# Sparse attention and gated feed-forward: one piece per pair for values and next scores, with the scores in the gate's and value's banks

## The chip, the cores and the metric

The kernel runs on one core of one Trainium2 chip, in one launch. The metric is the device time of that launch in microseconds (us). TensorE does the matrix products (PE in the profile; PEld is its loading of weights), VectorE (DVE), ScalarE (ACT) and GpSimd (POOL) work element by element, and SyncE (SP) starts DMA transfers. Matmuls write to PSUM, which has eight banks of 512 fp32 columns; the other operands are in SBUF.

## The reference

Eight batches of eight heads attend over 576 positions. Four heads see the last 32 positions ("local"), four see every 32nd ("strided"). The result feeds a gated layer without a routing step.

```python
rel = pos[:, None] - pos[None, :]
mask_local = (rel >= 0) & (rel < 32)
mask_strided = (rel >= 0) & (pos[None, :] % 32 == pos[:, None] % 32)
scores = np.where(masks, q @ k.T / sqrt(64), -1e9)          # per head
attn = softmax(scores)
x = (attn @ v), heads side by side: [4608 tokens, 512]
out = (sigmoid(x @ w_gate) * (x @ w_val)) @ w_out           # 512 -> 1536 -> 512
```

All data is fp32.

## The kernel before

**Feed-forward.** The 4608 tokens are nine blocks of 512. Block `k` below 8 holds the first 512 tokens of batch `k`; block 8 holds the 64 that are left over of each batch. The hidden size 1536 is twelve chunks `f` of 128. Each chunk takes three *rounds* on TensorE: gate (`g`), value (`v`) and outputs (`o`). Every operand is split into a high and a low part (`xh`/`xl`, `wh`/`wl`, `hh`/`hl`), and three products stand for one; so a gate or value round is 4 x 3 = 12 matmuls of 128x128 by 512 columns, and an output round is 4 token groups `i` x 3 = 12 matmuls too. Gate and value have one PSUM bank each, `g` and `v`, and no second one. The four output accumulators fill two pairs of banks, `o0` (`i` = 0, 1) and `o1` (`i` = 2, 3), over all twelve chunks. The last pair of banks, `a`, is for attention.

Behind a gate round ScalarE takes tanh and exp of `g` (tiles `t`, `e`), behind a value round VectorE multiplies the sigmoid together with `v` (`e`, line 410, the only reader of the bank `v`; then `t`, line 411), ScalarE rounds the result to `hh` and VectorE takes the rest, `hl`. Line 386 clears the sign bit of `t`. The output round of a chunk stands one chunk later: gate 5, value 5, outputs 4, gate 6 and so on. When the twelfth chunk of a block is summed, ScalarE copies accumulators 0 and 2 and VectorE 1 and 3 into the buffers `ost` and `l0` (one each), and SP stores them (lines 432 to 443).

**Attention.** A *pair* is two heads of one batch, four pairs (steps 0 to 3) a batch; steps 0 and 2 are local, 1 and 3 strided. A pair's functions have letters: `Q` and `V` load, `Z` takes room, `S` computes the scores (lines 208 to 214; 40 or 24 small matmuls), `F` adds the mask and takes off the maximum, `E` exp, `N` the sum and the scaling, `B` transposes in eight pieces of 32 rows on VectorE, `X` is the product with the values (line 289), `H`, `L` and `R` split the result into `xh` and `xl` of that batch's block and keep the 64 left-over tokens.

**Order.** The first two batches' attention, block 0 and the preparation of the weights follow a table written by hand. From block 1 on, `block` sets TensorE's order: while block `k` is in its feed-forward (`k` = 1 to 6), the four pairs of batch `k + 1` are worked on in eight *pieces* between rounds. Behind gate 0, 3, 6 and 9 stand a pair's scores, behind value 2, 5, 8 and 11 its values. Both use the banks `a`. TensorE keeps the order in which the code is written; for the other engines a scheduler chooses the order when the program is built, and each then works its queue off in that order.

Of the kernel before, what the change touches and what calls it, by code (L numbers as in the profile page):

```python
# [9 lines left out]
F32 = mybir.dt.float32  # L10
F32R = mybir.dt.float32r
# [3 lines left out]
ALU = mybir.AluOpType  # L15
# [28 lines left out]
NF = DF // P  # L44
BANK = 512
BY_PE = 2
AT = (0, 7)
LATE = NF - 1

BANKS = {  # L50
# [33 lines left out]
def attention_then_glu(ctx, tc, qk_l, qk_s, v_l, v_s, w_all, consts, out):  # L84
# [21 lines left out]
    def x_tiles(b):  # L106
        xs[b] = [(odd if b % 2 else work).tile([P, NC, TB], F32R, tag=t, name=f"{t}{b}") for t in ("xh", "xl")]
# [56 lines left out]
    def pair(b, step, space):  # L164
# [30 lines left out]

        todo = {}

        def score(sc):
            qk = tiles["qk"]

            m = LB if local else QB
            for n in range(ns * (P // m)):
                s, g = divmod(n, P // m)
                q = n % (NBL if local else NG)
                for j in range(2):
                    d = slice(j * D, (j + 1) * D)
                    q0, k0 = (q * LB, S + q * LB) if local else (q * GS, SK + q * GS)
                    nc.tensor.matmul(  # L208
                        sc[g * m : (g + 1) * m, j * BANK + s * kk : j * BANK + (s + 1) * kk],
                        qk[d, q0 : q0 + m],  # L210
                        qk[d, k0 : k0 + kk],
                        start=True,
                        stop=True,
                    )
            todo["soft"] = sc.rearrange("p (j n) -> p j n", j=2)[:, :, : ns * kk]

        def soft():
            sc = todo["soft"]
            prob, row, by_row = rows()
            if local:  # L220
                to = tiles["sb"][:, : 2 * ns * kk].rearrange("p (j n) -> p j n", j=2)
                nc.vector.tensor_tensor(to, sc, mask_l.broadcast_to([P, 2, ns * kk]), op=ALU.add)
            else:
                for j in range(2):
                    to, sv = prob[:, j * ns : (j + 1) * ns], sc[:, j].rearrange("p (t k) -> p t k", k=kk)
                    nc.vector.tensor_tensor(to, sv, mask_s.broadcast_to([P, ns, kk]), op=ALU.add)
            nc.vector.tensor_reduce(row, prob, axis=AX.X, op=ALU.max)
            nc.vector.tensor_tensor(prob, prob, by_row, op=ALU.subtract)  # L228

# [106 lines left out]
    def bank(tag, name):  # L336
        return ps.tile([P, 2 * BANK], F32, tag=tag, name=name)

    def attention(b):

        x_tiles(b)
        left_over(b)
        for step in range(4):
            do = pair(b, step, work)
            do["Q"](), do["V"](), do["Z"]()
            do["S"](bank("a", f"s{b}_{step}"))
            do["F"](), do["E"](), do["N"](), do["B"]()
            yield
            do["X"](bank("a", f"x{b}_{step}"))
            do["H"](), do["L"](), do["R"]()  # L350
            yield

    def split_rest():
# [34 lines left out]
    def glu_val(k, f, v=None):  # L388
        if v is None:
            v = ps.tile([P, BANK], F32, tag="v", name=f"v{k}_{f}")  # L390
            products(v, k, f, 1)
        if k == 0:
            e, t = hs[k, f], work.tile([P, TB], F32, tag="t", name=f"t{k}_{f}")
        else:
            t, e = hs[k, f]
        hh = work.tile([P, TB], F32R, tag="hh", name=f"hh{k}_{f}", bufs=2)
        hl = work.tile([P, TB], F32R, tag="hl", name=f"hl{k}_{f}", bufs=2)
        hs[k, f] = (hh, hl)
        half = 1.0 if k == 0 else 0.5
# [10 lines left out]
        nc.vector.scalar_tensor_tensor(e, e, 1.0, v, op0=ALU.min, op1=ALU.mult)  # L410
# [5 lines left out]
    def glu_out(k, f):  # L416
        hh, hl = hs.pop((k, f))
        if f == 0:
            two = [bank(f"o{n}", f"o{k}_{n}") for n in range(NTT // 2)]
            acc[k] = [two[i // 2][:, i % 2 * BANK : (i % 2 + 1) * BANK] for i in range(NTT)]  # L420
        for i in range(NTT):
            for n, (h, w) in enumerate(((hh, wh[f][2]), (hh, wl[f][2]), (hl, wh[f][2]))):
                nc.tensor.matmul(  # L423
                    acc[k][i],
                    h[:, i * P : (i + 1) * P],
                    w,
                    start=f == 0 and n == 0,
                    stop=f == NF - 1 and n == 2,
                )
        if f < NF - 1:  # L430
            return
        for i, o in enumerate(acc.pop(k)):
            ob = (work if i % 2 else odd).tile([P, DM], F32, tag="l0" if i % 2 else "ost", name=f"ob{k}_{i}")
            if i % 2:
                nc.vector.tensor_copy(ob, o)  # L435
            else:
                nc.scalar.copy(ob, o)
            if k < B:
                nc.sync.dma_start(out[k * S + i * P : k * S + (i + 1) * P, :], ob)
            else:  # L440
                for n in range(P // REST):
                    at = (i * P // REST + n) * S + TB
                    nc.sync.dma_start(out[at : at + REST, :], ob[n * REST : (n + 1) * REST, :])

    def block(k, f, pend, last):
        for slot in range(3):
            if slot == 0:
                glu_gate(k, f)
            elif slot == 1:
                glu_val(k, f)  # L450
            elif last:
                glu_out(*last)
            if (3 * f + slot) % 9 in AT:
                next(pend, None)

    for f in range(LATE):
        weight_tiles(f)
# [55 lines left out]

    with tc.manual_schedule(engines={mybir.EngineType.PE}):
        last = (0, NF - 1)
        for k in range(1, NB):
            pend = attention(k + 1) if k + 1 < B else iter(())
# [5 lines left out]
            for _ in pend:  # L523
                pass
        glu_out(*last)


def _layouts(q, k, v, w_gate, w_val, w_out):
# [80 lines left out]
```

## Time and profile before

| | |
|---|---|
| median of 3 runs | 1005.47 us (1004.60 to 1009.63) |
| the profiled execution | 1005.63 us, of it 1003.8 us span |
| TensorE busy | 975.5 us (97%) |
| VectorE busy | 589.0 us (59%) |
| ScalarE busy | 319.8 us (32%) |
| TensorE in the chain that ended last | 91% of the span |
| mean granted TensorE clock | 0.996 |
| one outputs matmul of 512 columns, mean | 394 ns, started every 227 ns |
| large matmuls in one round | 12, 2.72 us |

A matmul's row is longer than the distance to the next matmul's start, since they overlap; the chain of waits counts a round from the end of the round before to its own last matmul's end. "MATMUL ... x72" for values counts each fp32 matmul as two. The profile's DVE rows of one softmax are spread by source line: 222 or 226 mask (local, strided), 227 maximum, 228 subtraction, 236 sum, 237 and 238 reciprocal, 239 scaling, 261 transposes.

### The profile page before, as it was taken

To read this page: it belongs to the slowest core of one execution; us is meant where nothing else is said; L and a number is where in the kernel's file an instruction comes from. 1 tells how busy PE (TensorE), PEld (TensorE's weight loads), DVE (VectorE), ACT (ScalarE), POOL (GpSimd) and SP (SyncE) were. 2 spreads that over 40 slices of the span, in tenths; PEclk is the share of its full clock that TensorE was granted. 3 is DMA by queue.
4 is the path that set the end of the run, shared out by engine and by line. 5 is a ranking of instruction groups with operands and counts; after the bars stand their busy time and mean duration, and the time that the engine had idled before them with its cause. 6 is when DMAs were issued, how large, how long until landed. Compare 5 with 4: busy or idle time off the path is not lost.

```text
span 1003.8 us, 18124 instructions
## 1 busy us (share of the span) xinstructions
PE 975.5 (97%) x7840; PEld 794.7 (79%) x7840; DVE 589.0 (59%) x1042; ACT 319.8 (32%) x635; POOL 5.3 (1%) x20
## 2 busy tenths in 40 slices
PE   4999999999999999999999999999999999999996
PEld 3787878888888888888888888888888888888885
DVE  5888876666666566656665666666665633333222
ACT  3887853222322222222222232223222322222221
POOL 0000000000000000000000000000000000000000
PEclk9999999999999999999999999999999999999999
DMA  6666632111211121101210121112110010000001
GB/s 235 231 184 208 216 109 74 35 51 41 94 41 52 41 73 62 51 21 48 84 46 31 41 94 41 52 41 83 52 52 17 1 43 1 0 7 36 1 1 42
DMA packets 19871, 66.02 MB, mean 66 GB/s; under 512 B 2256, under 2 KB 2384, under 8 KB 19792
## 3 DMA queue, kind: packets, MB, share of 16 engines
q1 hardware_dynamic: 18352, 59.28, 18.3%
q10 hardware_dynamic: 1440, 5.59, 1.7%
q8 instruction: 61, 1.00, 0.4%
q14 instruction: 18, 0.15, 0.0%
HBM read 55.42 MB, written 9.44 MB: 65 GB/s over the span
## 4 chain that ended last, share of the span: by engine, by line
PE 91%; DMA 3%; DVE 3%; ACT 2%; issue 0%; SPq 0%; ACTq 0%; DVEq 0%
PE v L369 29%; PE o L423 28%; PE g L369 27%; PE x L289 3%; PE s L208 3%; DMA raw<-in_w_all 1%; DMA qk<-in_qk_l 1%; DMA qk<-in_qk_s 1%; ACT high L139 1%; PE gv L369 0%; DVE high L149 0%; ACT low L143 0%; DVE mx L236 0%; DVE w L162 0%; ACT pt L269 0%
## 5 line engine op out<-in xcount | busy, mean ns | idle before, releaser
L423 PE MATMUL o<-w,hh 128*128 128x512 f32 x864 | 270.2, 394 | 0.0
L369 PE MATMUL v<-xh,w 128*128 128x512 f32 x784 | 262.8, 395 | 0.0
L369 PE MATMUL g<-xh,w 128*128 128x512 f32 x784 | 258.4, 390 | 0.0
L423 PEld LDWEIGHTS o<-w,hh 128*128 128x128 f32 x864 | 159.6, 188 | 35.2 <-DVE ob L435 2.1
L369 PEld LDWEIGHTS v<-xh,w 128*128 128x128 f32 x784 | 148.1, 189 | 32.9
L369 PEld LDWEIGHTS g<-xh,w 128*128 128x128 f32 x784 | 147.2, 188 | 30.9
L386 DVE TENSOR_SCALAR t<-t 128x512 int32<-128x512 int32 x96 | 41.0, 427 | 219.7 <-ACT t L383 218.9
L423 PE MATMUL o<-w,hl 128*128 128x512 f32 x432 | 168.4, 390 | 0.0
L369 PE MATMUL v<-xl,w 128*128 128x512 f32 x392 | 153.8, 392 | 0.0
L369 PE MATMUL g<-xl,w 128*128 128x512 f32 x392 | 152.7, 390 | 0.3 <-DVE xl L324 0.3
L402 ACT ACTIVATE hh<-t 128x512 fp32r<-128x512 f32 x108 | 68.3, 633 | 258.1 <-DVE t L411 256.3
L383 ACT ACTIVATE t<-g 128x512 f32<-128x512 f32 x96 | 57.4, 598 | 265.2 <-PE g L369 265.2
L410 DVE SCALAR_TENSOR_TENSOR e<-e,v 128x512 f32<-128x512 f32 x96 | 65.8, 686 | 91.2 <-PE v L369 91.2
L261 DVE STREAM_TRANSPOSE pt<-sb 32x320 f32<-32x320 f32 (+1 forms) x192 | 103.0, 536 | 3.1
L405 DVE SCALAR_TENSOR_TENSOR hl<-t,hh 128x512 fp32r<-128x512 f32 x108 | 74.6, 691 | 48.5 <-ACT hh L402 48.5
L423 PEld LDWEIGHTS o<-w,hl 128*128 128x128 f32 x432 | 81.1, 188 | 17.6 <-DVE hl L405 0.4
L369 PEld LDWEIGHTS g<-xl,w 128*128 128x128 f32 x392 | 73.6, 188 | 15.8 <-DVE xl L324 0.8
L369 PEld LDWEIGHTS v<-xl,w 128*128 128x128 f32 x392 | 74.0, 189 | 14.3
L411 DVE SCALAR_TENSOR_TENSOR t<-t,e 128x512 f32<-128x512 f32 x96 | 66.5, 692 | 3.3
L384 ACT ACTIVATE e<-g 128x512 f32<-128x512 f32 x96 | 57.0, 594 | 0.0
L232 ACT ACTIVATE sb<-sb 128x640 f32<-128x640 f32 (+1 forms) x32 | 23.8, 744 | 69.5 <-DVE sb L228 69.5
L289 PEld LDWEIGHTS x<-pt,vv 64*64 64x64 f32 (+1 forms) x1856 | 34.8, 140 | 13.7 <-issue 9.7
(60 smaller groups left out, 655.2 us busy)
## 6 DMA issues: line engine op xcount, KB each, us to landing
raw<-in_w_all SPq DMA_DIRECT2D x36, 512.0 KB, 4.2
qk<-in_qk_s SPq DMA_DIRECT2D x14, 599.0 KB, 4.2
vv<-in_v_l SPq DMA_DIRECT2D x13, 640.0 KB, 4.0
qk<-in_qk_l SPq DMA_DIRECT2D x14, 592.0 KB, 3.8
out<-ob SPq DMA_DIRECT2D x32, 256.0 KB, 2.0
vv<-in_v_s SPq DMA_DIRECT2D x13, 384.0 KB, 3.2
vv<-in_v_l ACTq DMA_DIRECT2D x3, 640.0 KB, 5.8
qk<-in_qk_s ACTq DMA_DIRECT2D x2, 599.0 KB, 4.2
```

Of the source, the lines that this page charges most:

```text
L208: nc.tensor.matmul(sc[g * m : (g + 1) * m, j * BANK + s * kk : j * BANK + (s + 1) * kk], qk[d, q0 : q0 + m], qk[d, k0 : k0 + kk], start=Tr ...
L261: nc.vector.transpose(dst[to : to + LB, :, col : col + LB], src[rows : rows + LB, :, h * LB : (h + 1) * LB])
L289: nc.tensor.matmul(xp[j * D : (j + 1) * D, r * BANK + (u * per + g) * m : r * BANK + (u * per + g + 1) * m], v[rows, (u * per + g) * P + j ...
L369: nc.tensor.matmul(o, w, x, start=first and n == 0, stop=last and n == len(todo) - 1)
L383: nc.scalar.activation(t, g, AF.Tanh, scale=0.5)
L384: nc.scalar.activation(e, g, AF.Exp)
L386: nc.vector.tensor_scalar(ti, ti, 0x7FFFFFFF, None, op0=ALU.bitwise_and)
L402: nc.scalar.activation(hh, t, AF.Copy, scale=half)
L405: nc.vector.scalar_tensor_tensor(hl, t, half, hh.bitcast(F32), op0=ALU.mult, op1=ALU.subtract)
L410: nc.vector.scalar_tensor_tensor(e, e, 1.0, v, op0=ALU.min, op1=ALU.mult)
L411: nc.vector.scalar_tensor_tensor(t, t, 1.0, e, op0=ALU.add, op1=ALU.mult)
L423: nc.tensor.matmul(acc[k][i], h[:, i * P : (i + 1) * P], w, start=f == 0 and n == 0, stop=f == NF - 1 and n == 2,)
```

## The change

1. `attention` is now one generator over all 24 pairs. A piece holds a pair's values and then the next pair's scores. It stands in blocks 1 to 6 at chunks 2, 5, 8 and 11, behind the output round of the chunk before, and that chunk's own output round follows at once. The first scores stand alone, the last values too.
2. All scores but the first go to two single banks with the tags `g` and `v`, one head each, so the banks `a` are for values alone. The local mask is added in two instructions, one for each bank. `V` is loaded behind the mask and the next pair's `Q` behind the transposes.
3. So the output round of chunk 3 (6, 9) is no longer ahead of piece and gate: behind a piece come outputs 2, gate 3, value 3, gate 4, value 4, outputs 3. `hh` and `hl` have three buffers instead of two.
4. In block 8 the output rounds of chunks 10 and 11 are done together, accumulator by accumulator, behind outputs 9; each accumulator is copied and stored when it is done, from four different buffers, and the last one in two halves by ScalarE and VectorE.

```diff
-            todo["soft"] = sc.rearrange("p (j n) -> p j n", j=2)[:, :, : ns * kk]
+            todo["soft"] = [x.rearrange("p (j n) -> p j n", n=BANK)[:, :, : ns * kk] for x in sc]
...
+    def attention():
+        todo = [(b, step) for b in range(BY_PE, B) for step in range(4)]
+        ahead, now = pair(*todo[0], work), None
+        ahead["Q"]()
+        for n, (b, step) in enumerate(todo + [(B, 0)]):
+            if now:
+                of, p = todo[n - 1]
...
+                now["X"](bank("a", f"x{of}_{p}"))
+                now["H"](), now["L"](), now["R"]()
+            if b < B:
+                now = ahead
+                now["Z"]()
+                if n == 0:
+                    now["S"](bank("a", f"s{b}_{step}"))
+                else:
+                    now["S"](*(ps.tile([P, BANK], F32, tag=t, name=f"s{b}_{step}_{t}") for t in "gv"))
+                now["F"](), now["V"](), now["E"](), now["N"](), now["B"]()
+                if n + 1 < len(todo):
+                    ahead = pair(*todo[n + 1], work)
+                    ahead["Q"]()
+            yield
...
-        hh = work.tile([P, TB], F32R, tag="hh", name=f"hh{k}_{f}", bufs=2)
-        hl = work.tile([P, TB], F32R, tag="hl", name=f"hl{k}_{f}", bufs=2)
+        hh = work.tile([P, TB], F32R, tag="hh", name=f"hh{k}_{f}", bufs=3)
+        hl = work.tile([P, TB], F32R, tag="hl", name=f"hl{k}_{f}", bufs=3)
...
+    def give_out(k, i, cut=slice(0, DM), by=None):
+        tag = ("ost", "l0", "t", "e")[i if k == B else i % 2]
...
+    def glu_out(k, *fs):
...
         for i in range(NTT):
+            for f in fs:
+                out_products(k, f, i)
+            if k == B and fs[-1] == NF - 1 and i < NTT - 1:
+                give_out(k, i)
...
+        if k == B:
+            give_out(k, NTT - 1, slice(0, DM // 2), nc.scalar.copy)
+            give_out(k, NTT - 1, slice(DM // 2, DM), nc.vector.tensor_copy)
+        else:
+            for i in range(NTT):
+                give_out(k, i)
...
         last = (0, NF - 1)
+        pend = attention()
         for k in range(1, NB):
...
             for f in range(NF):
-                block(k, f, pend, last)
-                last = (k, f)
...
+                glu_gate(k, f)
+                glu_val(k, f)
+                if last and (k, f) != (B, NF - 2):
+                    glu_out(*last)
+                    last = None
+                if (k, f) == (1, 0):
+                    next(pend)
+                if k + 1 < B and f % 3 == 2:
+                    next(pend)
+                    glu_out(k, f)
+                else:
+                    last = last or (k, f)
+        glu_out(B, NF - 2, NF - 1)
```

**VectorE around a strided pair's softmax in block 3** (pair 1 of batch 4: tiles `sb4_1`, `mx4_1`, `pt4_1`; `e3_3`, `t3_3`, `hl3_3` belong to chunk 3 of block 3). Before:

```order
L226 TENSOR_TENSOR sb4_1_4016<-s4_1_4019,cst_61 128x6x54
L227 TENSOR_REDUCE mx4_1_4017<-sb4_1_4016 128x12 [waits DVE_49]
L228 TENSOR_TENSOR sb4_1_4016<-sb4_1_4016,mx4_1_4017 128x12x54 [waits DVE_49]
L410 SCALAR_TENSOR_TENSOR e3_3_4007<-e3_3_4007,v3_3_4062 128x512 [waits PE_49,Activation_49]
L411 SCALAR_TENSOR_TENSOR t3_3_4008<-t3_3_4008,e3_3_4007 128x512 [waits DVE_49]
L236 TENSOR_REDUCE mx4_1_4017<-sb4_1_4016 128x12 [waits Activation_49]
L405 SCALAR_TENSOR_TENSOR hl3_3_4076<-t3_3_4008,hh3_3_4075 128x512 [waits Activation_49]
```

And now, at the same pair:

```order
L326 TENSOR_TENSOR xl4_3967<-x4_0_3968,xh4_3966 128x512 [waits Activation_49]
L228 TENSOR_TENSOR sb4_1_4008<-s4_1_g_4011,cst_61 128x6x54 [waits PE_49]
L228 TENSOR_TENSOR sb4_1_4008<-s4_1_v_4012,cst_61 128x6x54 [waits PE_49]
L229 TENSOR_REDUCE mx4_1_4009<-sb4_1_4008 128x12 [waits DVE_49]
L230 TENSOR_TENSOR sb4_1_4008<-sb4_1_4008,mx4_1_4009 128x12x54 [waits DVE_49]
L238 TENSOR_REDUCE mx4_1_4009<-sb4_1_4008 128x12 [waits Activation_49]
L239 TENSOR_SCALAR mx4_1_4009<-mx4_1_4009 128x12 [waits DVE_49]
L240 RECIPROCAL mx4_1_4009<-mx4_1_4009 128x12 [waits DVE_49]
L241 TENSOR_TENSOR sb4_1_4008<-sb4_1_4008,mx4_1_4009 128x12x54 [waits DVE_49]
L263 STREAM_TRANSPOSE pt4_1_4048<-sb4_1_4008 32x12x32 [waits DVE_49]
L263 STREAM_TRANSPOSE pt4_1_4048<-sb4_1_4008 32x12x32 [waits Pool_49]
L263 STREAM_TRANSPOSE pt4_1_4048<-sb4_1_4008 32x12x32 x6
```

The next two rows now are chunk 3's sign bit and the multiply that reads its value bank, which stood in the middle of the softmax before:

```order
L400 TENSOR_SCALAR t3_3_4085<-t3_3_4085 128x512 [waits Activation_49]
L424 SCALAR_TENSOR_TENSOR e3_3_4084<-e3_3_4084,v3_3_4089 128x512 [waits PE_49,Activation_49]
L425 SCALAR_TENSOR_TENSOR t3_3_4085<-t3_3_4085,e3_3_4084 128x512 [waits DVE_49]
L419 SCALAR_TENSOR_TENSOR hl3_3_4103<-t3_3_4085,hh3_3_4102 128x512 [waits Activation_49]
L400 TENSOR_SCALAR t3_4_4122<-t3_4_4122 128x512 [waits Activation_49]
```

All 23 merged pieces have this order; at the first chunk of a block two output copies of the block before stand in it as well, one ahead of the sum and one ahead of the transposes.

**TensorE at the end** (`o8_0` is the pair of banks of accumulators 0 and 1, `o8_1` that of 2 and 3). Before, the last round:

```order
L423 MATMUL o8_0_8358<-w11_2_1766,hh8_11_8844 128x512 [waits Activation_49]
L423 MATMUL o8_0_8358<-w11_2_1766,hh8_11_8844 128x512
L423 MATMUL o8_0_8358<-w11_2_1766,hl8_11_8845 128x512 [waits DVE_49]
L423 MATMUL o8_0_8358<-w11_2_1766,hh8_11_8844 128x512 x2
L423 MATMUL o8_0_8358<-w11_2_1766,hl8_11_8845 128x512
L423 MATMUL o8_1_8359<-w11_2_1766,hh8_11_8844 128x512 x2
```

Now, from accumulator 0's last three matmuls to the first of accumulator 2:

```order
L433 MATMUL o8_0_8392<-w11_2_1766,hh8_11_8866 128x512 [waits Activation_49]
L433 MATMUL o8_0_8392<-w11_2_1766,hh8_11_8866 128x512
L433 MATMUL o8_0_8392<-w11_2_1766,hl8_11_8867 128x512 [waits DVE_49]
L433 MATMUL o8_0_8392<-w10_2_94,hh8_10_8829 128x512 [waits Activation_49]
L433 MATMUL o8_0_8392<-w10_2_94,hh8_10_8829 128x512
L433 MATMUL o8_0_8392<-w10_2_94,hl8_10_8830 128x512
L433 MATMUL o8_0_8392<-w11_2_1766,hh8_11_8866 128x512 x2
L433 MATMUL o8_0_8392<-w11_2_1766,hl8_11_8867 128x512
L433 MATMUL o8_1_8393<-w10_2_94,hh8_10_8829 128x512 x2
```

The fourth row is accumulator 1's first matmul: it has a wait for ScalarE, although its operand was already used for accumulator 0. Accumulator 3's first matmul has the same.

More of the change, by code (lines that the diff above doesn't have):

```diff
@@ L46 @@
 BY_PE = 2
-AT = (0, 7)
 LATE = NF - 1
@@ L196, in pair, with score @@
         todo = {}
-        def score(sc):
+        def score(*sc):
             qk = tiles["qk"]
@@ L208, in score @@
                     nc.tensor.matmul(
-                        sc[g * m : (g + 1) * m, j * BANK + s * kk : j * BANK + (s + 1) * kk],
+                        sc[j % len(sc)][g * m : (g + 1) * m, j // len(sc) * BANK + s * kk : j // len(sc) * BANK + (s + 1) * kk],
                         qk[d, q0 : q0 + m],
@@ L337, in bank @@
         return ps.tile([P, 2 * BANK], F32, tag=tag, name=name)
[L339 to L350, printed above, removed]
+    def attention():
[5 more added lines that the diff above has]
+                of, p = todo[n - 1]
+                if p == 0:
+                    x_tiles(of)
+                    left_over(of)
+                now["X"](bank("a", f"x{of}_{p}"))
[11 more added lines that the diff above has]
+                    ahead["Q"]()
             yield
@@ L414, in attention_then_glu, with out_products @@
     acc = {}
-    def glu_out(k, f):
-        hh, hl = hs.pop((k, f))
-        if f == 0:
+    def out_products(k, f, i):
+        hh, hl = hs[k, f]
+        for n, (h, w) in enumerate(((hh, wh[f][2]), (hh, wl[f][2]), (hl, wh[f][2]))):
+            nc.tensor.matmul(
+                acc[k][i],
+                h[:, i * P : (i + 1) * P],
+                w,
+                start=f == 0 and n == 0,
+                stop=f == NF - 1 and n == 2,
+            )
+    def give_out(k, i, cut=slice(0, DM), by=None):
+        tag = ("ost", "l0", "t", "e")[i if k == B else i % 2]
+        if (k, i) not in given:
+            given[k, i] = (odd if tag == "ost" else work).tile([P, DM], F32, tag=tag, name=f"ob{k}_{i}")
+        ob, o = given[k, i], acc[k][i]
+        if by is None:
+            by = (nc.scalar.copy, nc.vector.tensor_copy)[i % 2]
+        by(ob[:, cut], o[:, cut])
+        if k < B:
+            nc.sync.dma_start(out[k * S + i * P : k * S + (i + 1) * P, cut], ob[:, cut])
+        else:
+            for n in range(P // REST):
+                at = (i * P // REST + n) * S + TB
+                nc.sync.dma_start(out[at : at + REST, cut], ob[n * REST : (n + 1) * REST, cut])
+    given = {}
+    def glu_out(k, *fs):
+        if fs[0] == 0:
             two = [bank(f"o{n}", f"o{k}_{n}") for n in range(NTT // 2)]
@@ L421, in glu_out @@
         for i in range(NTT):
[L422 to L430, printed above, removed]
-            return
[L432 to L454, printed above, removed]
+            for f in fs:
+                out_products(k, f, i)
+            if k == B and fs[-1] == NF - 1 and i < NTT - 1:
+                give_out(k, i)
+        if fs[-1] < NF - 1:
+            return
+        if k == B:
[4 more added lines that the diff above has]
+                give_out(k, i)
     for f in range(LATE):
@@ L520, in attention_then_glu @@
             for f in range(NF):
-                block(k, f, pend, last)
-                last = (k, f)
-            for _ in pend:
-                pass
-        glu_out(*last)
+                glu_gate(k, f)
[8 more added lines that the diff above has]
+                    glu_out(k, f)
+                else:
+                    last = last or (k, f)
+        glu_out(B, NF - 2, NF - 1)
 def _layouts(q, k, v, w_gate, w_val, w_out):
```

9 lines of the change are left out of this document (5 added, 4 removed).

## The prediction

> **What bounds the kernel now.** I read the page first, then the chain of waits, then the timelines of the engines around one pair, and last the end.
>
> ```profile
> span 1003.8 us, 18124 instructions
> PE 975.5 (97%) x7840; PEld 794.7 (79%) x7840; DVE 589.0 (59%) x1042; ACT 319.8 (32%) x635; POOL 5.3 (1%) x20
> PE 91%; DMA 3%; DVE 3%; ACT 2%; issue 0%; SPq 0%; ACTq 0%; DVEq 0%
> 315.08:422.97 107.89, 107.89 (x921) 87.77 (x921) 67.60 (x121) 27.94 (x59) 0.68 (x2) 1.00 0.16 53
> ```
>
> TensorE is the bound: 91% of the chain, and in the stretch of one whole token block (the last row) it is busy for all 107.89 us at full clock. That leaves two things to gain: what TensorE loses between kinds of matmuls, and the end. It also means that every wait put on TensorE is paid in full. The chain, around both kinds of pair (start, us, what):
>
> ```profile
> 226.45 1.28 PE x L289 x72
> 227.73 2.95 PE o L423 x12
> 230.68 2.72 PE g L369 x12
> 233.40 0.85 PE s L208 x48
> 234.25 2.94 PE v L369 x12
> ...
> 253.51 0.84 PE x L289 x44
> 254.35 2.94 PE o L423 x12
> ...
> 260.01 0.97 PE s L208 x64
> 260.98 2.99 PE v L369 x12
> ```
>
> A round of twelve large matmuls takes 2.72; the round behind a piece of small ones takes 2.94 to 2.99. So each piece has a toll of 0.22 to 0.27, 0.24 on average.
>
> **The saving.** Before, 48 pieces stand between rounds. Now there are 25: the first scores, 23 merged pieces, the last values. 23 tolls fall away: 23 x 0.24 = 5.5 us at most. Whether the change from values to scores inside a piece has a toll of its own no row shows (between 0 and 0.24). It turns out not to matter, because of what comes next.
>
> **The new wait.** The scores now sit in the banks of gate and value. Behind a merged piece TensorE runs: outputs, gate, value, gate, value, with no outputs between the two value rounds. The second value round writes the bank that the first filled, so it has to wait until VectorE has multiplied the first one out (`e`, line 410). On VectorE the order puts that multiply behind the entire softmax of the new pair: split, two mask additions, maximum, subtraction, sum, scaling and eight transposes. Before, the multiply of the first value round stood in the middle of the softmax. I time this queue from VectorE's and ScalarE's own rows before (start, us, ...):
>
> ```profile
> 228.54 0.57 ACT L320 CAST xh<-x 128x512 fp32r<-128x512 f32 x1
> 229.27 0.68 DVE L324 TENSOR_TENSOR xl<-x,xh 128x512 fp32r<-128x512 f32 x1
> 233.50 0.60 ACT L383 ACTIVATE t<-g 128x512 f32<-128x512 f32 x1 [3.29 <-PE g L369]
> 234.47 0.89 DVE L226 TENSOR_TENSOR sb<-s,cst 128x324 f32<-128x324 f32 x2
> 237.12 0.75 ACT L232 ACTIVATE sb<-sb 128x648 f32<-128x648 f32 x1 [2.54 <-DVE sb L228]
> 238.64 0.82 DVE L236 TENSOR_REDUCE mx<-sb 128x12 f32<-128x648 f32 x1
> 240.03 0.17 DVE L237 TENSOR_SCALAR mx<-mx 128x12 f32<-128x12 f32 x1
> 241.36 4.65 DVE L261 STREAM_TRANSPOSE pt<-sb 32x384 f32<-32x384 f32 x8
> 246.38 0.68 DVE L410 SCALAR_TENSOR_TENSOR e<-e,v 128x512 f32<-128x512 f32 x1
> ...
> 214.27 4.12 DVE L261 STREAM_TRANSPOSE pt<-sb 32x320 f32<-32x320 f32 x8
> 218.77 0.68 DVE L410 SCALAR_TENSOR_TENSOR e<-e,v 128x512 f32<-128x512 f32 x1
> ...
> 255.61 0.70 ACT L320 CAST xh<-x 128x288 fp32r<-128x288 f32 x3
> 256.34 0.82 DVE L324 TENSOR_TENSOR xl<-x,xh 128x288 fp32r<-128x288 f32 x3
> ```
>
> Pair of strided scores behind local values (12 merged pieces), in us from the start of the piece:
> - Values end at 1.28. ScalarE follows a TensorE end by 0.10 (gate ends 230.68 + 2.72 = 233.40, tanh starts 233.50), so its cast starts at 1.38, VectorE's split 0.73 later (228.54 to 229.27) at 2.11, and the mask additions a step of 0.61 to 0.68 later at 2.75. The scores have ended by then (1.28 + 0.85).
> - Mask additions to exponential: 234.47 to 237.12, 2.65. Exponential and step: 0.78. Sum and step: 0.86. Scaling: 240.03 to 241.36, 1.33. Transposes, sign bit and all, up to the multiply: 241.36 to 246.38, 5.02. The multiply: 0.69. Together 11.33: the value bank is free at 14.08.
> - TensorE comes there at 1.28 + 0.85 + 2.95 + 3 x 2.72 = 13.24.
>
> How fast TensorE goes on is seen where one round already waits for VectorE, at an output copy:
>
> ```profile
> 164.19 2.96 PE o L423 x12
> 164.72 0.69 DVE L435 COPY ob<-o 128x512 f32<-128x512 f32 x1
> ```
>
> The copy ends at 165.41 and the round at 167.15; the six matmuls that waited take 6 x 0.227 = 1.36, so in the chain's count they begin at 165.79, 0.38 after the copy. The second value round thus begins at 14.08 + 0.38 = 14.46 instead of 13.24: **1.2 us lost, 12 times, 14.6 us.**
>
> Local scores behind strided values (11 pieces): values end at 0.84, cast at 0.94, split at 1.67, mask additions at 2.48; the transposes are 0.52 shorter (214.27 to 218.77 is 4.50), so 10.8 up to the end of the multiply, 13.28, and TensorE begins at 13.66. It comes there at 0.84 + 0.97 + 2.97 + 8.16 = 12.94: **0.7 us, 11 times, 7.9 us.** A toll inside the piece would make TensorE come later and wait less; the sum stays.
>
> Five of these 11 stand at a block's end, with two output copies on VectorE ahead of the multiply. The first (0.69) fits into the wait for the exponential. The second stands ahead of the transposes and waits for the first one's store:
>
> ```profile
> 157.43 0.59 ACT L437 COPY ob<-o 128x512 f32<-128x512 f32 x1 [0.90 <-PE o L423]
> 160.23 0.59 ACT L437 COPY ob<-o 128x512 f32<-128x512 f32 x1 [1.69 <-DMA out<-ob]
> ```
>
> A buffer is back 2.2 us after its copy ended (158.02 to 160.23). VectorE's first copy ends near 5.8, the store is done at 8.0, and the scaling ends at 8.1: so only the copy itself, 0.65 us, **5 times, 3.3 us.**
>
> Nothing is late twice: behind the delayed value round come outputs and gate, 5.4 us, before the next value round asks for its bank, and VectorE's queue has only that round's own multiplies left by then. The rest I cost at nothing: the three-deep `hh` and `hl` let one round stay open and fit. Values' and scores' loads leave when their buffers come free, a pair (27 us) ahead of need, against 4 us to landing (row below); ScalarE, 32% busy, hides its part. The first scores move behind the outputs but stay in their own bank. SP takes the same loads, now within 1 us of each other.
>
> ```profile
> vv<-in_v_l SPq DMA_DIRECT2D x13, 640.0 KB, 4.0
> ```
>
> **The end.** Before:
>
> ```profile
> 993.71 0.40 PE L423 MATMUL o<-w,hl 128*128 128x512 f32 x1
> 994.15 0.59 ACT L437 COPY ob<-o 128x512 f32<-128x512 f32 x1 [2.01 <-PE o L423]
> 995.09 0.39 PE L423 MATMUL o<-w,hl 128*128 128x512 f32 x1
> 997.82 0.59 ACT L437 COPY ob<-o 128x512 f32<-128x512 f32 x1 [3.08 <-DMA out<-ob]
> 999.20 0.69 DVE L435 COPY ob<-o 128x512 f32<-128x512 f32 x1 [3.74 <-DMA out<-ob]
> L443 SPq DMA_DIRECT2D out<-ob x8: 466/562/595, 994.8 to 1000.4; - x8
> ```
>
> The third and fourth copies wait 3.08 and 3.74 us for a buffer; four buffers end that. But the first copy began at 994.15, when the second accumulator's last matmul had ended (993.71 + 0.40): waits go by the pair of banks. Now that copy stands between the two accumulators' matmuls, and in the order TensorE's next matmul waits for ScalarE. Each such stop costs (0.39 - 0.23) + 0.04 + 0.59 + 0.19 for going on = 0.98 us, and there are two. The last matmul then ends 1.9 later, at 997.4; the halves are copied one after the other (the same pair of banks) by 998.2, and four stores of 0.56 each leave from 997.8, the last at 999.5, against 1000.4 before: **0.9 us gained.** [...]
>
> **Sum.** 14.6 + 7.9 + 3.3 - 5.5 - 0.9 = +19.4 us. The profiled execution took 1005.63 (span 1003.8), the median of three 1005.47; so 1025, and I take 1024 since VectorE's steps without a wait between them overlap by up to 0.08. Half a per cent, 5 us, is about what a measurement of this kernel can tell from no change.
>
> **Rivals.**
> - *The softmax stays hidden* (faster). It decides at 1.2 us: were VectorE's queue that much shorter per pair, no value round would wait, and 5.5 + 0.9 would be gained, 999. Against it: all 11.3 us are rows of VectorE one behind the other, and only the wait for the exponential has slack. Chance 0.07.
> - *Half hidden* (same): local pairs hidden and strided ones at half price, 7 + 3 - 6 = +4, 1009. Chance 0.05.
> - *Stores behind loads* (slower still). At a block's end two loads of some 600 KB now leave 1 us apart, just ahead of the stores; if a store lands 2 us later, VectorE's second copy and the next block's tanh behind ScalarE's are late, 5 x 2 = 10 us, 1034. For it: 4 us per load; against: the second load leaves 2.4 us before the first store. Chance 0.08.
> - *The clock drops in the stalls.* [...] Here TensorE was idle from 133.45 to 139.24 and the round of 140.09 ran at full speed all the same, so 0.01.
>
> ```profile
> 132.56 0.89 PE s L208 x48
> ...
> 139.24 0.85 PE t L247 x6
> 140.09 2.77 PE g L369 x12
> ```
>
> **Chances and range.** Likeliest, a stall in each merged piece: 0.79, 1014 to 1031 (each stall 0.4 us shorter or 0.3 longer). With 0.08 for 1034 above and 0.12 below, 1014 to 1031 is also my range. Faster 0.07, same 0.05, slower 0.88.
>
> **What would show it.** In the chain, second value rounds behind merged pieces start 1.2 (strided) and 0.7 us late with VectorE's multiply as releaser, and a block takes some 111.5 us instead of 107.89; TensorE's rounds behind pieces at 2.95 number 25. At the end two stops of about 1 us released by the output copy, and the last store leaving 2.5 us after the last matmul began (5.3 before). I am wrong if those rounds start without a wait, or if VectorE's transposes no longer stand ahead of the multiply.

## The result, and the profile after

The changed kernel takes 1032.86 us (median, 1031.55 to 1033.40), the kernel before beside it 1006.33: a ratio of 1.0254, with an interval from 1.0232 to 1.0276. The forecast was 1024, with a range up to 1031: the direction and the mechanism came, the size was 8 to 9 us short. The profiled execution has a span of 1031.6 against 1003.8, 27.8 us more.

The page's head, and from the table of waits (engine and line that wait, for what: us in total, times, longest) those of the value rounds:

```profile
span 1031.6 us, 18069 instructions
PE 64%; DVE 23%; DMA 6%; ACT 5%; issue 2%; SPq 0%; ACTq 0%; DVEq 0%
...
PE v L383 <- DVE e L424: 21.1, 23, 1.8
```

VectorE, 3% of the chain before, is now 23%, and there are 23 waits, one for each merged piece. The chain (start, us, what) over the three kinds of merged piece:

```profile
232.96 1.22 PE x L291 x69
...
246.92 3.02 PE v L383 x12
...
260.81 0.84 PE x L291 x44
...
264.24 0.60 ACT ob L449
264.85 4.48 DMA out<-ob
269.43 0.60 ACT ob L449
...
275.87 4.60 PE v L383 x12
...
291.38 1.22 PE x L291 x69
...
319.26 0.86 PE x L291 x44
332.49 3.02 PE v L383 x12
...
346.39 1.22 PE x L291 x69
```

From one piece to the next there are 27.85 us behind strided scores (232.96 to 260.81), 27.13 behind local ones (319.26 to 346.39), and 30.57 behind local ones at a block's end (260.81 to 291.38). The second value round starts 13.96, 13.23 and 15.06 after its piece. The block's end is the new thing: between the first output copy and the third lies a store of 4.48 us, and the value round that was held up takes 4.60 instead of 3.02. Granted clock and DMA in that place (stretch; us, then busy time of PE, PEld, DVE, ACT and POOL with counts, then the clock, the DMA share and GB/s):

```profile
264.00:265.00 1.00, 1.00 (x6) 0.81 (x6) 0.93 (x3) 0.59 (x1) 0.00 (x0) 1.00 0.85 352
267.00:268.00 1.00, 1.00 (x6) 0.84 (x5) 0.90 (x4) 0.00 (x0) 0.00 (x0) 1.00 0.88 344
...
276.00:277.00 1.00, 1.00 (x3) 0.81 (x4) 0.54 (x1) 0.42 (x1) 0.00 (x0) 0.51 0.00 0
```

While the store is under way the DMA engines are 0.85 to 0.88 busy in these two stretches, with two loads of some 600 KB that left just ahead of it (at 261.69 and 262.67), and behind the stall the clock falls to half (0.51).

The end:

```profile
1016.35 4.09 PE o L433 x18
1020.46 0.59 ACT ob L449
1021.10 3.03 PE o L433 x12
1024.15 0.59 ACT ob L449
1024.79 1.68 PE o L433 x6
```

Two stops on an output copy, as forecast. To see where the time went I cut each run into three parts: up to the first merged piece (before: the same values), from there to the last values alone, and from there to the end. In the changed order one output round of 2.72 us stands ahead of the piece that stood behind it before; I count it to the last part. Each row of the table is one profiled execution; that of e2_nomax was the slowest of its five runs.

| kernel | up to the first piece | merged pieces | last part | span |
|---|---|---|---|---|
| before | 172.6 | 620.4 | 210.8 | 1003.8 |
| after | 175.3 | 645.9 | 210.4 | 1031.6 |
| e1_early | 177.1 | 614.0 | 209.6 | 1000.8 |
| e2_nomax | 175.8 | 613.5 | 210.4 | 999.7 |
| e3_middle | 171.7 | 644.8 | 211.7 | 1028.2 |
| e4_end | 175.1 | 620.5 | 209.6 | 1005.2 |
| f1_four | 174.0 | 634.7 | 210.4 | 1019.1 |
| f2_queue | 175.2 | 641.3 | 210.3 | 1026.8 |
| f3_banks | 175.7 | 645.7 | 208.6 | 1030.1 |
| g3_first | 176.0 | 614.0 | 207.8 | 997.8 |

The first part runs the same order in after, e3_middle, f1_four, f2_queue and f3_banks, and it lies between 171.7 and 175.7. The third buffers of `hh` and `hl` are a rival to plain spread here: e3_middle and f1_four have two and are the shortest (171.7 and 174.0), the others have three. Against it stand g2_plain, with three and 171.6, and e4_end, which has three and whose ten runs lost nothing; so I count the 2.7 us as spread, and this is not shown. Of the 27.8 us, 25.5 come from the middle.

### The profile page after: what moved, and what is told of

Read it like the earlier page. It is cut to its first block, busy times and chain, and to the rows that moved or that the text cites. A ratio compares the mean times of both kernels' runs of the same rounds, so it can differ in the third digit from the quotient of the medians.

```text
span 1031.6 us, 18069 instructions
## 1 busy us (share of the span) xinstructions
PE 981.7 (95%) x7840; PEld 798.0 (77%) x7840; DVE 597.1 (58%) x1053; ACT 323.3 (31%) x636; POOL 6.7 (1%) x20
## 4 chain that ended last, share of the span: by engine, by line
PE 64%; DVE 23%; DMA 6%; ACT 5%; issue 2%; SPq 0%; ACTq 0%; DVEq 0%
PE v L383 22%; PE o L433 21%; PE g L383 15%; DVE pt L263 9%; PE x L291 3%; DMA raw<-in_w_all 2%; DMA out<-ob 2%; DVE sb L241 2%; DVE mx L238 2%; DVE sb L230 2%; DVE mx L229 2%; ACT sb L234 2%; DVE e L424 1%; DVE xl L326 1%; DVE sb L228 1%
## 5 line engine op out<-in xcount | busy, mean ns | idle before, releaser
L383 PE MATMUL v<-xh,w 128*128 128x512 f32 x784 | 265.8, 400 | 21.1 <-DVE e L424 21.1
L383 PEld LDWEIGHTS v<-xh,w 128*128 128x128 f32 x784 | 150.3, 192 | 62.3 <-DVE e L424 30.8
L326 DVE TENSOR_TENSOR xl<-x,xh 128x512 fp32r<-128x512 f32 (+1 forms) x64 | 24.1, 419 | 40.5 <-ACT xh L322 40.4
L291 PEld LDWEIGHTS x<-pt,vv 64*64 64x64 f32 (+1 forms) x1856 | 35.1, 141 | 13.7 <-issue 9.3
```

What stands on the lines that cost most here:

```text
L291: nc.tensor.matmul(xp[j * D : (j + 1) * D, r * BANK + (u * per + g) * m : r * BANK + (u * per + g + 1) * m], v[rows, (u * per + g) * P + j ...
L326: nc.vector.tensor_tensor(dst(xs[b][1]), src, dst(xs[b][0]).bitcast(F32), op=ALU.subtract)
L383: nc.tensor.matmul(o, w, x, start=first and n == 0, stop=last and n == len(todo) - 1)
```

## The experiments

My theory was the prediction's: the second value round waits for a multiply that VectorE does only behind the next pair's whole softmax. The rivals: the merged piece is dear in itself, whatever VectorE does; the new end costs what the middle does not; and, once the profile was seen, the stores behind loads and the clock as causes of the dear block ends.

### e1_early: the multiply moved forward

VectorE's order is written by hand too. The first value round's multiply stands behind half of the transposes (the two `yield`s let a value round in), and the last output copy of a block behind the next block's first multiply. The splitting of block 8's left-over tokens moves forward too, from block 8 to block 7. Of the edit, the main lines:

```diff
...
-                now["F"](), now["V"](), now["E"](), now["N"](), now["B"]()
+                now["F"](), now["V"](), now["E"](),
+                if n:
+                    yield
+                    now["N"](), now["B"](range(2))
+                    yield
+                    now["B"](range(2, 4))
+                else:
+                    now["N"](), now["B"]()
...
                 glu_val(k, f)
+                if f == 0 and 1 < k < B:
+                    give_out(k - 1, 3)
+                if 1 < k < B - 1 and f == 0 or 0 < k < B - 1 and f in (3, 6, 9):
+                    next(pend)
...
```

> The changed kernel with VectorE's queue in written order from block 1 on: the first value round's multiply stands behind four of the eight transposes instead of behind all of them, and at a block's end the second output copy stands behind that multiply. Nothing is left out. The queue theory (all stalls come from the multiply standing behind the whole softmax, and at the blocks' ends also behind the store): strided pairs fall from 27.85 us a piece period to 26.8, local ones from 27.1 to 26.5, block ends from 29.8 to about 27; 12 x 1.0 + 6 x 0.6 + 5 x 2.8 = 30 us less than the changed kernel, so about 1003, 3 below the kernel before. The rival (the merged piece itself is dear: shapes that alternate on TensorE, scores that alternate between two banks): the periods stay, 1030 to 1033.

It took 1001.96 us, a ratio of 0.9966 (0.9945 to 0.9986). VectorE's rows behind the first strided pair, and the chain (the second fence):

```profile
241.25 2.31 DVE L265 STREAM_TRANSPOSE pt<-sb 32x384 f32<-32x384 f32 x4
243.94 0.68 DVE L433 SCALAR_TENSOR_TENSOR e<-e,v 128x512 f32<-128x512 f32 x1
```

```profile
233.06 1.22 PE x L293 x69
...
259.77 0.84 PE x L293 x44
...
286.58 1.22 PE x L293 x69
313.29 0.84 PE x L293 x44
339.80 1.22 PE x L293 x69
```

The multiply now ends 11.56 us after its piece (243.94 + 0.68 - 233.06); in the changed kernel the round that waits for it starts only at 13.96. No second value round is late: 26.71 us behind strided scores (233.06 to 259.77), 26.51 behind local ones (313.29 to 339.80; 26.50 in most). These are the periods without a stall. The merged piece itself is no loss, and the rival that it is dear falls. The block end shown still takes 26.81, and one block end of this run took 27.16.

### e2_nomax: a shorter queue

The changed kernel, its order left to the scheduler, without maximum and subtraction for batches 2 to 7.

```diff
-            nc.vector.tensor_reduce(row, prob, axis=AX.X, op=ALU.max)
-            nc.vector.tensor_tensor(prob, prob, by_row, op=ALU.subtract)
+            if b < BY_PE:
+                nc.vector.tensor_reduce(row, prob, axis=AX.X, op=ALU.max)
+                nc.vector.tensor_tensor(prob, prob, by_row, op=ALU.subtract)
```

> The changed kernel without the subtraction of the row maximum for batches 2 to 7 (scores here are small, so exp needs none): two of VectorE's steps, 1.7 us, fall out of the queue ahead of the multiply. Queue theory: the value bank is free 1.7 us earlier, which is more than the stall of a strided (1.0) or a local pair (0.6), so these vanish, 12 x 1.0 + 6 x 0.6 = 16 us; the scheduler also puts the second output copy behind the transposes, so block ends lose part of their 2.8 as well, another 5 to 14 us: 1003 to 1012. The rival (dear pieces): TensorE's periods stay, 1030 to 1033.

996.67 us, 0.9916 (0.9888 to 0.9944): better than I expected. VectorE is busy for 557.4 us instead of 597.1, 1.65 less per pair, which is more than the 1.1 that strided pairs lacked, so nothing waits there, and at the block ends the scheduler now put the second output copy behind the transposes. The chain's pieces (26.71 and 26.58 apart):

```profile
231.75 1.22 PE x L292 x69
...
258.46 0.84 PE x L292 x44
...
285.04 1.22 PE x L292 x69
```

### f4_control: the same on the kernel before

The same edit on the kernel before.

> The kernel before, with the maximum and its subtraction left out for blocks 2 to 7 (as in e2_nomax). Theory: VectorE is hidden there, so its 40 us less of work change nothing: 1003 to 1008, and what e2_nomax gained is the merged pieces' tolls and the new end. Rival: part of VectorE's queue is paid in the kernel before too, and this one reaches 995 to 1001.

1006.12 us, 0.9991 (0.9969 to 1.0014): no difference. 40 us less on VectorE are worth nothing where it is hidden. What e2_nomax gains is the change's own gain, with its stall taken away.

### e3_middle and e4_end: the two halves of the change

e3_middle has the changed middle with the old end and two buffers for `hh` and `hl`; e4_end the old middle with the new end and three buffers.

```diff
e3_middle, against after:
...
-        glu_out(B, NF - 2, NF - 1)
+        glu_out(*last)
e4_end, against before:
...
-        glu_out(*last)
+        glu_out(B, NF - 2, NF - 1)
```

> The change without its new end: merged pieces and scores in the gate's and value's banks, but the old last round with two buffers for hh and hl. Both theories: merged pieces as in the changed kernel, +25.6 us over the kernel before from the first merged piece to the last values, the end as before. If the 2.9 us that the first stage took longer in the changed kernel come from the third buffers (other addresses), this run has a first stage as before, block 1's first gate round at 149.4 us; if they are chance of the loads it is anywhere between 148 and 154. Total 1032 or 1029 to 1036.

> The kernel before with the new end and the three buffers for hh and hl alone. The middle as before (a block 107.9 us). The end: two stops of TensorE for the output copies, 0.9 us each, against the two buffer waits that fall away; half a microsecond gained as in the changed kernel, 1005 to 1007. If the third buffers lengthen the first stage, 2.9 us more: 1008.5 to 1009.

e3_middle: 1028.21 us, 1.0236 (1.0182 to 1.0289). e4_end: 1004.75, 0.9974 (0.9952 to 0.9997). All of the loss is the middle's. By the table the new end gains 1.2 us on the old middle (210.8 to 209.6) and 1.3 on the new one (211.7 to 210.4); 0.9 was forecast.

### f1_four and f2_queue: why the block ends are dear

f1_four is e3_middle with four output buffers, so that no copy waits for a store. f2_queue is the changed kernel with the stores of blocks 1 to 7 issued on ScalarE's queue.

```diff
f1_four, against e3_middle:
-            ob = (work if i % 2 else odd).tile([P, DM], F32, tag="l0" if i % 2 else "ost", name=f"ob{k}_{i}")
+            tag = ("ost", "l0", "ob2", "ob3")[i]
+            ob = (odd if tag[0] == "o" else work).tile([P, DM], F32, tag=tag, name=f"ob{k}_{i}")
f2_queue, against after:
-            nc.sync.dma_start(out[k * S + i * P : k * S + (i + 1) * P, cut], ob[:, cut])
+            (nc.sync if k == 0 else nc.scalar).dma_start(out[k * S + i * P : k * S + (i + 1) * P, cut], ob[:, cut])
```

> The changed order of the middle with the old end and two hh/hl buffers (as in e3_middle), and now a buffer of its own for each of a block's four outputs, so that no output copy waits for a store. Theory (stores behind loads): the block-end periods fall from 29.8 to about 27.9 us (27.6 to 28.5), since only the two copies themselves are left in VectorE's queue, and the clock no longer falls behind them; e3_middle's 1028.2 falls by 5 x 1.9 + about 3 for the two rounds at half clock, to 1014 to 1020. Rival (the block ends are dear for another reason, the loads or the two copies): they stay at 29 or more and the time is 1025 to 1029.

> The changed kernel with the stores of blocks 1 to 7 issued on ScalarE's queue in place of SyncE's, on which the loads are. If a store is late because it stands behind the two loads of its own queue, it lands in 2.0 to 2.5 us, block-end periods fall to about 28 us, and the time is 1020 to 1024. If it is late because the 16 DMA engines are shared with the loads whatever the queue, it still takes 3.5 us or more, the periods stay at 29 or more, and the time is 1029 to 1034.

f1_four: 1018.57 us, 1.0129 (1.0085 to 1.0174), some 9.6 less than e3_middle. VectorE at the first block end, and the chain there:

```profile
264.46 1.28 DVE L450 COPY ob<-o 128x512 f32<-128x512 f32 x2
265.66 0.81 DVE L238 TENSOR_REDUCE mx<-sb 128x10 f32<-128x640 f32 x1
```

```profile
259.59 0.86 PE x L291 x44
...
273.01 3.04 PE v L383 x12
...
286.93 1.22 PE x L291 x69
```

With the buffers free, the scheduler put both copies ahead of the sum, mostly into the time in which VectorE waits for the exponential anyway. The five block ends take 27.34, 27.36, 28.06, 27.32 and 27.59 us, mean 27.53, against 29.54 in e3_middle (28.77, 30.92, 28.73, 30.51, 28.79), and no value round is slow. So the buffer that waits for its store makes the block ends dear. The copies themselves cost about 0.4 at each block end (27.53 - 27.13).

f2_queue: 1026.91 us, 1.0211 (1.0167 to 1.0255), between the two expectations. The DMA row for the first store of the first block end in f2_queue (name, queue, KB, us to landing), and the row in which the first stores of the third block end are issued:

```profile
out<-ob ACTq DMA_DIRECT2D x1, 256.0 KB, 4.6
...
490.09 0.83 ACTq L451 DMA_DIRECT2D out<-ob  x2
```

Away from the loads most stores land in 2.0 to 2.2 us. On a queue without loads the first store was just as late at two block ends (4.6 both times, against 4.5 and 4.9). At the other three it took 3.0 to 3.2, but there it left 1.1 us after its copy had ended, behind the exponential in ScalarE's own queue (the copy ended at 488.97). Counted from the end of the copy, the first stores landed after 4.1 to 4.6 us here and after 4.5 to 5.0 in the changed kernel. So the order in SyncE's queue is worth some 0.3 us, and the rest of the delay is there without it; what is left, as my estimate from these times, is how busy the DMA engines are (0.85 to 0.88 in the changed kernel); no run tried that alone. The five periods are 29.07, 29.47, 28.71, 28.51 and 28.59, mean 28.87. In the changed kernel they are 30.57, 29.42, 29.05, 30.84 and 29.08, and without the 1.58 us that each of the two slow rounds costs (4.60 - 3.02), 29.16 in the mean: the queue itself brings 0.3 each, which agrees. The rest of f2_queue's gain is that no round in it fell to half clock.

### f3_banks: the two stops at the end

The last block's accumulators 0, 1, 2 and 3 stand in three pairs of banks (`o0`, `o1`, `a`, and `o0` again), so that no copy reads the pair that TensorE writes next.

```diff
+            if k == B:
+                two.append(bank("a", f"o{k}_a"))
+            at = ((0, 0), (1, 0), (2, 0), (0, 1)) if k == B else ((0, 0), (0, 1), (1, 0), (1, 1))
-            acc[k] = [two[i // 2][:, i % 2 * BANK : (i % 2 + 1) * BANK] for i in range(NTT)]
+            acc[k] = [two[n][:, half * BANK : (half + 1) * BANK] for n, half in at]
```

> The changed kernel with the last block's four accumulators spread over three pairs of banks, so that the copy of one never stands in the pair into which TensorE writes next. If the two stops at the end come from pairs shared by copy and matmul, both vanish: from the start of the last 18-matmul stretch to the end of the span 13.3 to 13.7 us instead of 15.25, and 1029.5 to 1032 in all. If the stops have another cause (the copies' order, ScalarE), they stay near 0.9 each and the stretch at 15.2.

1030.70 us, 1.0238 (1.0184 to 1.0291), and the end in the chain:

```profile
1016.61 1.36 PE o L433 x6
1017.97 0.68 PE o_a L433 x3
1018.65 3.40 PE o L433 x15
1022.05 1.36 PE o_a L433 x6
1023.41 1.37 PE o L433 x6
```

The same 36 matmuls run without a stop, and from 1016.61 to the end of the span are 13.5 us, against 15.25 from 1016.35 in the changed kernel: 1.8 us for the two stops. The prediction had the two stops from a row of the kernel before, in which a copy waited for the neighbour bank's matmul (994.15). In the changed kernel too the copy read another bank than the one TensorE was to write, and only the tile of two banks was shared. With separate tiles there is no wait, and in the order shown above the wait is one for ScalarE that the program makes. Whether the memory would have let the copy and the matmuls run side by side in the two banks of one pair, no run here shows.

### g1_keepmax, g2_plain, g3_first: versions that beat both kernels

g1_keepmax is e1_early with f3_banks' end, and the fourth copy of block 0 moved behind the multiply of value round 1. g2_plain is e2_nomax with f3_banks' end. g3_first is e1_early with f3_banks' end, and in block 1 the first softmax is cut in two around a multiply.

```diff
g1_keepmax, against e1_early:
...
-                if f == 0 and 1 < k < B:
+                if f == 0 and 1 < k < B or (k, f) == (1, 1):
                     give_out(k - 1, 3)
...
g3_first, against e1_early:
-                if n:
-                    yield
+                yield
+                if n:
                     now["N"](), now["B"](range(2))
...
-                if 1 < k < B - 1 and f == 0 or 0 < k < B - 1 and f in (3, 6, 9):
+                if 1 < k < B - 1 and f == 0 or 0 < k < B - 1 and f in (3, 6, 9) or (k, f) == (1, 1):
                     next(pend)
...
```

> e1_early (VectorE's and TensorE's order written so that the first value round's multiply stands in the middle of the next pair's softmax) with the last block's accumulators in three pairs of banks (f3_banks) and the fourth copy of block 0 moved behind a later multiply. By the theory nothing is left but the gains: e1_early's span 1000.8, less 1.8 for the two stops at the end, less about 2.5 for its one stall and slow round in block 1: a span of 996 to 998 and a median near 998 (996 to 1001), 0.990 to 0.995 of before. Rival (moving waits about only makes new ones): no better than e1_early, 1000 to 1004.

> The changed kernel without the maximum and its subtraction for blocks 2 to 7 (as e2_nomax) and with the three pairs of banks at the end (f3_banks). If the two gains add up: e2_nomax's span 999.7 less 1.8, so 997 to 999, median 994 to 998, 0.988 to 0.993 of before. Rival: no better than e2_nomax (0.9916).

> e1_early with the last block's accumulators in three pairs of banks and, in block 1, the first softmax cut in two around the multiply of the second value round, the fourth copy of block 0 where e1_early has it. If g1_keepmax was slow by the move of that copy alone (it held the outputs' banks: the first merged piece began at 186.43 against 179.85 in e1_early), that piece now begins at 174 to 178, the end is 1.8 us shorter than in e1_early, and the span is 995 to 998, 0.990 to 0.995 of before, with the whole softmax kept. If the three pairs of banks do harm of their own here, it stays at 1001 or more.

g1_keepmax: 1005.46 us, 1.0008 (0.9992 to 1.0024), worse than e1_early. Its chain:

```profile
174.28 0.61 DVE ob L458
175.03 2.90 PE o L442 x6
...
186.43 1.22 PE x L293 x69
```

The copy that I moved held the banks in which the next block's outputs were to start; TensorE waited for it, and the first merged piece began at 186.43 against 179.85. The rest was as expected (its last part is 207.8). g3_first undoes that move: its first merged piece begins at 178.74, and it takes 995.45 us, 0.9880 (0.9856 to 0.9905), with the whole softmax. g2_plain takes 994.90, 0.9897 (0.9879 to 0.9915), without the maximum. Both beat the kernel before by about 1% and the changed one by some 3.5%.

### h1_long: longer gaps, and the clock

Two of the five block-end stalls of the changed kernel were followed by a round at half clock, and so were two in e3_middle and two in f3_banks. Cut into tenths of a microsecond, the clock of the changed kernel reads (columns as above):

```profile
276.00:276.10 0.10, 0.10 (x1) 0.10 (x2) 0.10 (x1) 0.00 (x0) 0.00 (x0) 0.64 0.00 0
...
279.40:279.50 0.10, 0.10 (x2) 0.10 (x1) 0.00 (x0) 0.00 (x0) 0.00 (x0) 0.80 0.00 0
...
613.90:614.00 0.10, 0.10 (x1) 0.10 (x2) 0.10 (x1) 0.00 (x0) 0.00 (x0) 0.73 0.00 0
```

A tenth at 0.64 is 0.03 at full and 0.07 at half clock, so the first fall is from 276.03 to 279.44: 3.41 us. The second begins at 613.95. The lengths of the stops do not tell which of them a fall follows. The five at block ends of the changed kernel are 1.80, 1.82, 1.76, 1.78 and 1.80 us long, and the clock fell behind the first and the fourth. In e3_middle it fell behind two of 1.80 and not behind a third of 1.80; in f3_banks it fell behind one of 1.82 and one of 1.81 and stayed full behind one of 2.60. This run makes all gaps longer: each maximum is computed three times.

```diff
-            nc.vector.tensor_reduce(row, prob, axis=AX.X, op=ALU.max)
+            for _ in range(1 if b < BY_PE else 3):
+                nc.vector.tensor_reduce(row, prob, axis=AX.X, op=ALU.max)
```

> The changed kernel with each pair's maximum computed three times instead of once for blocks 2 to 7, so that VectorE's queue is 1.7 us longer and TensorE's gaps grow: strided 0.85 to about 2.5 us, local 0.3 to about 2.0, block ends 1.8 to about 2.2 (there the store hides most). [...] Time 1033 + 33 for longer stalls + about 14 more drops of 1.6: 1087 (1080 to 1094). Rival (the length of the gap alone decides): all 23 drop, about 1099; or (chance, not the gap) two or three drop, about 1065.

1098.47 us, 1.0918 (1.0860 to 1.0977), the profiled span 1094.5 at a mean clock of 0.956. The time alone would speak for the rival, but my sum was short elsewhere: the gaps of four of the five block ends became 3.05 to 3.14 instead of 2.2, there were 18 falls, and two of them lasted 6.83 us instead of 3.41. No run had shown the "about 14 more drops" of the sum; with two in the changed kernel, the 18 are 16 more. The trace counts these 18 falls for 23 gaps, and length alone does not tell which gaps they follow. Three gaps (time at which TensorE goes on, ..., gap and releaser):

```profile
409.56 0.50 PE L384 MATMUL v<-xh,w 128*128 128x512 f32 x1 [3.14 <-DVE e L425]
...
439.15 0.80 PE L384 MATMUL v<-xh,w 128*128 128x512 f32 x1 [2.58 <-DVE e L425]
...
811.42 0.50 PE L384 MATMUL v<-xh,w 128*128 128x512 f32 x1 [2.57 <-DVE e L425]
```

Behind the first, the run's longest, the clock stayed full. With the second it was half from 438.74 on, 0.41 before TensorE went on. The third is 0.01 shorter than the second, and the clock stayed full. The 18 gaps with a fall are 1.89 to 3.11 long, the five without one 1.68, 1.90, 2.57, 2.58 and 3.14. So the rival that the length decides does not hold here; what decides was not shown.

## Why the prediction was right and where it failed

By its own terms, in us of the profiled execution. The price of a stall is the period in the changed kernel less the period without stalls in e1_early:

| term | forecast | measured |
|---|---|---|
| tolls saved | -5.5 | -8.4 (620.4 before; 12 x 26.71 + 11 x 26.50 = 612.0 without stalls) |
| strided scores, 12 stalls | +14.6 | +13.7 (12 x (27.85 - 26.71)) |
| local scores away from block ends, 6 stalls | +4.3 | +3.8 (6 x (27.13 - 26.50)) |
| local scores at block ends, 5 stalls | +3.6 + 3.3 | +16.5 (5 x (29.79 - 26.50)) |
| the end | -0.9 | -0.4 |
| up to the first merged piece | 0 | +2.7 |
| sum | +19.4 | +27.9 (span +27.8) |

**Right.** The wait is the one that was named, with its number (23), its releaser and its size: second value rounds began at 13.96 and 13.23 where 14.46 and 13.66 were forecast. Of this half microsecond VectorE's queue explains 0.1 to 0.2: the multiply behind the first strided pair ended 13.90 after its piece (246.18 + 0.68 - 232.96) instead of 14.08, that of the local pair after 13.18 instead of 13.28.

```profile
246.18 0.68 DVE L424 SCALAR_TENSOR_TENSOR e<-e,v 128x512 f32<-128x512 f32 x1
```

The rest is a matter of counting: the prediction put all of its 0.38 for going on ahead of the round, and here the round starts 0.06 behind the multiply and takes 3.02 instead of 2.72. The loss by period, 1.14 and 0.63, is close to the 1.22 and 0.72 forecast.

The saving was larger than the tolls, and the prediction's "at most" for its 5.5 us was wrong: without its stall a strided period is 26.71 where 27.06 stood before (226.45 to 253.51), 0.35 less and not 0.24. What the rest of it is was not tried. The 2.9 us saved beyond the forecast hide part of the misses below, so that the forecast came as near as it did is in part luck. e1_early, e2_nomax and f4_control show the cause: move or shorten VectorE's queue and the change gains, shorten it in the kernel before and nothing happens.

**Wrong: the block ends**, 16.5 instead of 6.9, which is more than the whole miss. The step that failed is "the store is done at 8.0, and the scaling ends at 8.1: so only the copy itself, 0.65 us". The 2.2 us for a store came from a place without loads. Here two loads of some 600 KB are just ahead of it, and over the five block ends VectorE's own store took 3.6 to 4.0 us, and ScalarE's first store, ahead of it, 4.5 to 4.9. At the block end shown, VectorE's first copy ended 5.55 after the piece (5.8 was forecast), but its store left at 266.40 and was done 9.2 after the piece instead of 8.0. The second copy began at 9.24, by the profile behind ScalarE's third copy, which had itself waited for ScalarE's store:

```profile
270.05 0.69 DVE L449 COPY ob<-o 128x512 f32<-128x512 f32 x1 [1.28 <-ACT ob L449]
```

This was the rival *stores behind loads* (1034, chance 0.08), which I had set aside because the second load leaves 2.4 us before the first store. But the landing time of the loads was on the page: 4 us for one of them. Two of them keep the DMA engines busy beyond the moment of the store (0.85 to 0.88 in the stretches above). By f1_four 27.53 of the 29.79 us remain when no copy waits for a store, so 2.3 us at each block end, 11.3 in all, hang on the store: 8.1 as waiting, and 3.2 as two slow rounds. The other 1.0 at each block end is the stall of a local pair, 0.6, and the copies, 0.4.

**Wrong: the clock.** The rival of the dropping clock had 0.01 since "TensorE was idle from 133.45 to 139.24". It was not. In the chain there is no TensorE piece between these times, but the chain had followed other engines. The windows of the kernel before show TensorE busy throughout from 134 to 139; the first of these five stretches (columns as above):

```profile
134.00:135.00 1.00, 1.00 (x6) 0.83 (x5) 0.96 (x2) 0.00 (x0) 0.00 (x0) 1.00 0.91 321
```

So there was no evidence against that rival. It came true in part: two of 23 stalls, of 1.80 and 1.78 us, were followed by a round at half clock, and these rounds took 4.60 and 4.61 us instead of 3.02.

**The end.** Its two stops of 0.9 and its gain of 1.2 to 1.3 came, a little above the 0.9. But the changed middle loses 0.9 in the last part (210.8 to 211.7 in e3_middle), and in the changed kernel 0.6 of it is a new wait that I had not seen, at the last values alone, where an output matmul waits for `hl`:

```profile
826.10 0.50 PE L433 MATMUL o<-w,hl 128*128 128x512 f32 x1 [0.59 <-DVE hl L419]
```

**Probably not of the change.** The 2.7 us of the first part lie within what kernels with the same order there differ by (171.6 to 175.8, g2_plain and e2_nomax included); that they are spread is likely and not shown. Without them the forecast would have been 5 to 6 us short.

## What to carry to other kernels

When a bank gets a second use, ask who frees it and what stands ahead of that instruction in its engine's queue; the remedy was the order on VectorE, not on TensorE. With it the same change gains 0.3% (e1_early), and 1.2% with three pairs of banks at the end and the first softmax cut as well (g3_first). A store's landing time holds only for its place (2.0 to 2.2 us away from the loads, 3.6 to 4.9 just behind them here): where the change moves loads, look for stores that leave within their landing time, and give the copies behind them a buffer of their own. A gap in the chain of waits is not an idle engine: ask the windows, and beside a stop of TensorE count the slow round that may follow it: here 2 of 5 stops of 1.76 to 1.82 us had one, 1.6 us each.

## What the runs showed of the hardware that was not expected

Behind some stops of TensorE of less than 2 us its clock was half for 3.41 us, and behind others of the same length it was not: it was half behind two of the five block-end stops of the changed kernel (1.76 to 1.82 us). These two are all but equally long:

```profile
275.87 0.68 PE L383 MATMUL v<-xh,w 128*128 128x512 f32 x1 [1.80 <-DVE e L424]
```

```profile
389.77 0.50 PE L383 MATMUL v<-xh,w 128*128 128x512 f32 x1 [1.82 <-DVE e L424]
```

Behind the first the clock was half from 276.03 to 279.44, and a value matmul took 0.63 us where it takes 0.40 at full clock; behind the second it stayed full. The fall cost 1.6 us of TensorE's time (4.60 - 3.02). Longer gaps were followed by a fall more often, in 18 of 23 cases in h1_long (1.68 to 3.14 us), but not the longest. What decides beside the length was not shown.

Ahead of 150 us, where small matmuls of the attention stand between the large ones, the clock fell in f4_control with less idle time ahead of it. Of the 3.41 us ahead of that fall TensorE was idle for 0.83 (3.41 - 2.58); most of the 80 matmuls in them are small:

```profile
125.80:129.21 3.41, 2.58 (x80) 2.17 (x81) 3.27 (x7) 1.97 (x4) 0.20 (x1) 1.00 0.49 159
```

Whether small matmuls count for less was not tried.
